# Moving the first pair's x and the third pair's keys in a fused attention and two-layer MLP kernel on one Trainium2 core

## The chip, the cores and the metric

The kernel runs on one core of one Trainium2 chip. The metric is device time in microseconds (us). Five engines work side by side, each on its own instructions in its own order: TensorE (PE, the matrix engine, whose weight loads are listed apart as PEld), VectorE (DVE), ScalarE (ACT), GpSimd (POOL) and SyncE (SP). SP issues nearly all DMAs here, GpSimd a few. A matrix product ends in PSUM, of which this program uses eight banks of 128 x 512 float32; the other engines read it there.

## The reference

```
k_sum = max of k over blocks of 32 keys;  v_sum = mean of v over the same blocks     (batch 2, heads 8, sequence 768, head size 64)
scores = [ q k^T / 8 where |i - j| < 16, else -1e9 ;  q k_sum^T / 8 + log 32 ]
a      = exp(scores - row maximum);  a = a / (row sum + 1e-9)
x      = a [v; v_sum], heads side by side                                             (1536 tokens x 512)
x      = ((x w_a) * (x w_b)) w_out                                                    (inner width 1536)
out    = leaky(x w_in) w_out2, leaky(h) = max(0.01 h, h)                              (inner width 2048)
```

All inputs and outputs are float32.

## The kernel before

**Attention.** Heads are taken two by two (`hp` 0 to 3). Queries are taken 256 at a time, and two such groups make a "pair" `i`. The 1536 tokens are three chunks of 512. The first chunk is pairs 0 to 3, and pair `i` there is head pair `i` of batch 0 with its first 512 queries; "first pair" is pair 0, "third pair" is pair 2. A head pair's keys are loaded once (`load_k`), transposed on TensorE and copied into `kts` by ScalarE, and VectorE takes the maximum of each block of 32 (`k_prep`, whose reduction is L623); GpSimd then copies the maxima beside the windows (L630). Per pair the steps are: `q_prep`, and twice `scores` (16 small products; then on VectorE a masked minimum, L684, and on ScalarE the exponential, L690), `normal` (three VectorE instructions, L699 to L701) and `p_transpose` (four transposes and a ScalarE copy, L715), and at last `pv`, the products with the values (L725). `pv` ends in x: ScalarE rounds the result to the first of two float32r parts (L735) and VectorE subtracts to get the second (L736). The values' windows come by `load_vw`, the block means by `v_sums`, `v_place` and `put_sums`.

**Products with weights.** Each large product is made three times (`mm3`, L743): high by high, high by low, low by high. A weight of 512 KB is loaded by `stage` into one of three buffers (`wst`) and made into two parts by a row of small steps (`convert`): on VectorE L388, on ScalarE the absolute value L394, on VectorE L400, L403 and L409, on ScalarE the high half L416, on VectorE the rest L419. `wc` and `wr`, the tiles between, have two buffers each; a buffer of `wst` is free after L409. The first four weights are two blocks of `w_a` and two of `w_b`, in the order a, b, a, b. As soon as a pair's x is there, `early` multiplies it with all four, into four banks of their own. The other four banks (t0 to t3) go round among the steps of attention.

**What sets the order.** `attention_ops` gives each step a place on a scale (8 per pair, `PER`; `PV` = 13 is where `pv` stands), and the steps are listed by it. After a listed product the loop sends out two more steps of the weights' conversion (`tick(2)`), and `first_weights` sends out all that its weight still needs. The list is the order of priority only: when the program is built, a planner with costs of its own puts each engine's instructions in order, and takes the first on the list among those that it thinks ready. `tc.issue_after(ins)` puts the instructions of its block behind `ins` in the order of the engine on which `ins` runs, if they run on that engine. Once built, the order is fixed. DMAs on SP are ordered in the same way.

## Time and profile before

| | us |
|---|---|
| median of 3 runs | 637.85 |
| lowest, highest | 636.07, 638.39 |
| the profiled execution | 635.28 |
| its span, first to last instruction | 633.4 |

| engine | busy us in the span |
|---|---|
| PE | 611.6 |
| DVE | 485.4 |
| ACT | 317.9 |
| POOL | 55.7 |

The profile is of one execution. A line of a timeline has the start, the duration, the engine, the line of the program, the operation, the tile written and the tiles read, and how many like instructions were merged; in brackets stands how long the engine was idle before it and what ended that. DMA lines (SPq) show the issue, not the transfer; the time to the landing is asked for apart. A busy TensorE isn't TensorE at its peak, since its instructions overlap and their ends are modelled. The clock column gives the share of full speed that TensorE was granted.

### The profile page before, as it was taken

To read this page: it belongs to the slowest core of one execution; us is meant where nothing else is said; L and a number is where in the kernel's file an instruction comes from. 1 tells how busy PE (TensorE), PEld (TensorE's weight loads), DVE (VectorE), ACT (ScalarE), POOL (GpSimd) and SP (SyncE) were. 2 spreads that over 40 slices of the span, in tenths; PEclk is the share of its full clock that TensorE was granted. 3 is DMA by queue.
4 is the path that set the end of the run, shared out by engine and by line. 5 is a ranking of instruction groups with operands and counts; after the bars stand their busy time and mean duration, and the time that the engine had idled before them with its cause. 6 is when DMAs were issued, how large, how long until landed. Compare 5 with 4: busy or idle time off the path is not lost.

```text
span 633.4 us, 9456 instructions
## 1 busy us (share of the span) xinstructions
PE 611.6 (97%) x3344; PEld 498.5 (79%) x3344; DVE 485.4 (77%) x1070; ACT 317.9 (50%) x707; POOL 55.7 (9%) x101
## 2 busy tenths in 40 slices
PE   6589999999999999999999999999999999999997
PEld 4467777777888888888888888877888888888886
DVE  4996987853996869986889999687588576885552
ACT  5677885752545425434453648475463434443320
POOL 5224010000000001202120102000000000000000
PEclk9899999999999999999999999999999999999999
DMA  8989757620124503736593327323133013030013
GB/s 200 257 208 199 160 116 177 191 72 24 45 71 145 136 15 94 139 120 146 142 222 102 89 80 166 95 64 109 35 99 100 14 54 99 1 99 1 0 68 132
DMA packets 81006, 67.85 MB, mean 107 GB/s; under 512 B 47360, under 2 KB 67840, under 8 KB 80960
## 3 DMA queue, kind: packets, MB, share of 16 engines
q1 hardware_dynamic: 75808, 57.95, 31.7%
q0 software_dynamic: 5152, 9.31, 8.8%
q8 instruction: 26, 0.43, 0.3%
q14 instruction: 20, 0.16, 0.1%
HBM read 52.82 MB, written 10.49 MB: 100 GB/s over the span
## 4 chain that ended last, share of the span: by engine, by line
PE 80%; DVE 5%; DMA 5%; ACT 4%; issue 3%; SPq 1%; POOL 1%; POOLq 0%; DVEq 0%; ACTq 0%
PE ps_t L743 34%; PE ps_c L743 17%; PE ps_a L743 12%; PE ps_b L743 11%; PE ps_t L670 2%; DMA wst<-in_moe_w_out_dram 2%; PE ps_t L725 1%; PE ps_t L711 1%; ACT pm L690 1%; DMA neg<-wc 1%; DMA wst<-in_moe_w_a_dram 1%; DVE wc L403 1%; DMA q<-in_q_dram 1%; DVE wc L409 1%; SPq L209 1%
## 5 line engine op out<-in xcount | busy, mean ns | idle before, releaser
L743 PE MATMUL ps_c<-wsp,hs 128*128 128x512 f32 x288 | 75.1, 390 | 1.4 <-ACT acc L860 1.0
L743 PE MATMUL ps_t<-wsp,hs 128*128 128x512 f32 x288 | 74.5, 389 | 0.0
L743 PE MATMUL ps_t<-ys,wsp 128*128 128x512 f32 x270 | 68.2, 389 | 0.0
L394 ACT ACTIVATE wc<-wst 128x512 f32<-128x512 f32 x68 | 45.3, 673 | 45.2 <-DVE wsp L419 17.8
L743 PEld LDWEIGHTS ps_c<-wsp,hs 128*128 128x128 f32 x288 | 53.9, 188 | 13.3 <-ACT acc L860 1.4
L871 DVE TENSOR_TENSOR hs<-h,hs 128x512 fp32r<-128x512 f32 x72 | 49.3, 687 | 18.6 <-ACT hs L870 18.3
L743 PEld LDWEIGHTS ps_t<-wsp,hs 128*128 128x128 f32 x288 | 54.1, 188 | 11.2
L743 PEld LDWEIGHTS ps_t<-ys,wsp 128*128 128x128 f32 x270 | 50.7, 188 | 10.5
L870 ACT CAST hs<-h 128x512 fp32r<-128x512 f32 x72 | 44.5, 621 | 26.0 <-DVE h L1134 18.4
L416 ACT CAST wsp<-wc 128x512 fp32r<-128x512 f32 x68 | 41.8, 620 | 30.6 <-DVE wc L409 30.6
L743 PE MATMUL ps_a<-x,wsp 128*128 128x512 f32 x186 | 51.2, 403 | 4.5 <-ACT x L735 4.1
L743 PE MATMUL ps_t<-x,wsp 128*128 128x512 f32 x222 | 53.2, 389 | 0.0
L743 PE MATMUL ps_b<-x,wsp 128*128 128x512 f32 x192 | 51.7, 398 | 0.0
L1086 DVE TENSOR_TENSOR h<-ps_t,h 128x512 f32<-128x512 f32 x56 | 37.6, 687 | 17.0 <-PE ps_t L743 16.7
L1022 ACT ACTIVATE h<-h 128x512 f32<-128x512 f32 x32 | 20.2, 632 | 57.5 <-DVE h L1086 57.4
L743 PEld LDWEIGHTS ps_t<-x,wsp 128*128 128x128 f32 x222 | 41.7, 188 | 8.6
L403 DVE SCALAR_TENSOR_TENSOR wc<-wc,wr 128x512 int32<-128x512 int32 x68 | 46.5, 686 | 0.7
L409 DVE SCALAR_TENSOR_TENSOR wc<-wst,wc 128x512 int32<-128x512 int32 x68 | 46.6, 686 | 0.6
L743 PEld LDWEIGHTS ps_a<-x,wsp 128*128 128x128 f32 x186 | 33.9, 188 | 13.4 <-ACT x L735 4.6
L419 DVE TENSOR_TENSOR wsp<-wc,wsp 128x512 fp32r<-128x512 f32 x56 | 38.7, 697 | 5.8 <-ACT wsp L416 5.8
L743 PE MATMUL ps_t<-hs,wsp 128*128 128x512 f32 x144 | 42.7, 389 | 0.0
L690 ACT ACTIVATE pm<-pm,nb 128x128 f32<-128x128 f32 x96 | 37.5, 393 | 10.1 <-DVE nb L684 10.0
(129 smaller groups left out, 1098.1 us busy)
## 6 DMA issues: line engine op xcount, KB each, us to landing
wst<-in_moe_w_out_dram SPq DMA_DIRECT2D x28, 512.0 KB, 3.4
wst<-in_moe_w_in_dram SPq DMA_DIRECT2D x16, 512.0 KB, 3.8
wst<-in_moe_w_a_dram SPq DMA_DIRECT2D x12, 512.0 KB, 4.8
wst<-in_moe_w_b_dram SPq DMA_DIRECT2D x12, 512.0 KB, 4.0
y<-acc POOLq DMA_DIRECT2D x16, 256.0 KB, 6.1
y<-acc SPq DMA_DIRECT2D x12, 256.0 KB, 2.3
neg<-wc POOLq DMA_DIRECT2D x12, 256.0 KB, 3.5
acc<-y SPq DMA_DIRECT2D x12, 256.0 KB, 3.1
```

The lines of the kernel that those rows point to most:

```text
L394: nc.scalar.activation(out=t["c"].bitcast(F32), in_=hi_w.bitcast(F32), func=AF.Abs, scale=2.0**-112)
L403: nc.vector.scalar_tensor_tensor(out=t["c"], in0=t["c"], scalar=3, in1=t["r"], op0=ALU.logical_shift_left, op1=ALU.bitwise_or,)
L409: nc.vector.scalar_tensor_tensor(out=t["c"], in0=hi_w, scalar=SIGN, in1=t["c"], op0=ALU.bitwise_and, op1=ALU.bitwise_or,)
L416: t["high"] = nc.scalar.copy(out=t["w"][:, 0], in_=t["c"].bitcast(F32))
L419: nc.vector.tensor_tensor(out=t["w"][:, 1], in0=t["c"].bitcast(F32), in1=t["w"][:, 0].bitcast(F32), op=ALU.subtract,)
L670: nc.tensor.matmul(out=ps[h, w, :], lhsT=qt[h, w * W : (w + 1) * W], rhs=kts[h, (g * G + w) * SC : (g * G + w) * SC + P], start=True, stop ...
L690: nc.scalar.activation(out=pm[:, w, :], in_=pm[:, w, :], func=AF.Exp, scale=-1.0, bias=nb[:, w : w + 1], accum_out=sm[:, w : w + 1],)
L743: nc.tensor.matmul(out=ps, lhsT=w(a), rhs=x(b), start=first and j == 0, stop=last and j == 2)
L870: pace["split"] = nc.scalar.copy(out=t[:, 0], in_=src)
L871: nc.vector.tensor_tensor(out=t[:, 1], in0=src, in1=t[:, 0].bitcast(F32), op=ALU.subtract)
L1022: nc.scalar.activation(out=h, in_=src, func=AF.Prelu, alpha=0.01)
L1086: nc.vector.tensor_tensor(out=out, in0=ps, in1=u, op=ALU.add)
```

## The change

- The third pair's keys (batch 0, `hp` 2) are loaded later in the list: after two of the first three weights, which were loaded as three in a row (the third follows the keys).
- Their transposes stand at 13.5 and 13.75 on the scale, behind the first pair's `pv` (they stood at 4 and 5); the fourth pair's, formerly at 13.5 and 13.75, at 14 and 14.25. On TensorE both go behind the last product of values so far.
- Their reductions go behind the subtraction that makes the low part of the first x, and so does the first instruction of the second pair's second `normal`.
- The absolute value (L394) of every weight after the first goes behind the rounding of the first x on ScalarE, where it went behind the placing of the block means.
- Before place 13 only the first weight is converted (five before). The other three of the first four are asked for at 13.5, behind the first `pv`, not at 13 in front of it.

```diff
-                    add(-22 if b > 0 and hp >= NP - 2 else -18, LOAD, load_k, b, hp)
+                    add(-22 if b > 0 and hp >= NP - 2 else -13.4 if (b, hp) == (0, 2) else -18, LOAD, load_k, b, hp)
                     for j in range(2):
-                        add(2 * m + j / 4 - 10.5 if (b, hp) == (0, NP - 1) else 2 * m + j - 12, PRODUCT, k_prep, b, hp, j)
+                        at = {(0, 2): j / 4 - 2.5, (0, 3): j / 4 - 10}.get((b, hp), 2 * m + j - 12)
+                        add(at, PRODUCT, k_prep, b, hp, j)
...
-            with tc.issue_after(pace["turned"].ins):
+            with tc.issue_after(pace["turned"].ins if i < 1 else pace["first x"].ins):
                 nc.scalar.activation(
                     out=t["c"].bitcast(F32), in_=hi_w.bitcast(F32), func=AF.Abs, scale=2.0**-112
                 )
...
-        with tc.issue_after(st["out"].ins) if (b, hp) == (0, NP - 1) else nullcontext():
+        with tc.issue_after(st["out"].ins) if b == 0 and hp >= 2 else nullcontext():
             for i in range(n * GT // P):
                 nc.tensor.transpose(
...
-        nc.vector.tensor_reduce(
-            out=ks_t[hp][:, g * GT // BLK : (g + n) * GT // BLK],
...
+        with tc.issue_after(st["low x"].ins) if (b, hp) == (0, 2) else nullcontext():
+            nc.vector.tensor_reduce(
+                out=ks_t[hp][:, g * GT // BLK : (g + n) * GT // BLK],
...
-        with behind(i == 0):
+        after = st["low x"].ins if (i, j) == (1, 1) else line[-1]
+        with tc.issue_after(after) if i == 0 or (i, j) == (1, 1) else nullcontext():
             nc.vector.tensor_scalar_add(sm, sm, 1.0e-9)
...
-            nc.scalar.copy(out=x[:, 0], in_=src)
-            nc.vector.tensor_tensor(
+            hi = nc.scalar.copy(out=x[:, 0], in_=src)
+            lo = nc.vector.tensor_tensor(
                 out=x[:, 1], in0=src, in1=x[:, 0].bitcast(F32), op=ALU.subtract
             )
+            if i == 0:
+                pace["first x"], st["low x"] = hi, lo
...
-    ops.append((2.5, LOAD, lambda: [stage() for _ in range(3)], 0))
+    ops.append((2.5, LOAD, lambda: [stage() for _ in range(2)], 0))
+    ops.append((2.7, LOAD, stage, 0))
     firsts = ((("a", 0), "a"), (("b", 0), "b"), (("a", 1), "c0"), (("b", 1), "c1"))
     for i, x in enumerate(firsts):
-        ops.append((PV, LOAD, lambda x=x: first_weights(*x), 0))
+        ops.append((PV if i < 1 else PV + 0.5, LOAD, lambda x=x: first_weights(*x), 0))
...
-            if o[1] == PRODUCT and o[0] >= PER+0.5 and (bg or cnt["conv"] < N_FIRST):
+            n_now = 1 if o[0] < PV else N_FIRST
+            if o[1] == PRODUCT and o[0] >= PER+0.5 and (bg or cnt["conv"] < n_now):
                 tick(2)
```

## Rows read from the trace of the kernel before

**Rows 1.** Page, part 1: busy us, share of the span, instructions
```profile
PE 611.6 (97%) x3344; PEld 498.5 (79%) x3344; DVE 485.4 (77%) x1070; ACT 317.9 (50%) x707; POOL 55.7 (9%) x101
```

**Rows 2.** Windows: length, busy us per engine (instructions), granted clock, DMA share, GB/s
```profile
12.00:32.00 20.00, 11.91 (x123) 9.07 (x121) 19.71 (x59) 13.64 (x48) 3.54 (x4) 0.91 0.91 241
...
34.00:47.30 13.30, 11.17 (x113) 8.52 (x112) 13.27 (x45) 10.55 (x35) 3.30 (x4) 1.00 0.79 195
47.30:62.60 15.30, 14.25 (x148) 10.94 (x147) 10.66 (x44) 11.03 (x42) 6.77 (x9) 1.00 0.93 199
62.60:82.00 19.40, 19.25 (x217) 15.37 (x215) 17.30 (x64) 15.81 (x55) 3.44 (x7) 1.00 0.71 154
```

**Rows 3.** Timeline of TensorE around the first large product
```profile
22.52 0.69 PE L725 MATMUL ps_t<-pt,vw 128*64 128x64 f32 x16 [0.99 <-ACT pt L715]
23.15 0.87 PE L612 MATMUL ps_t<-ident,k 128*128 128x128 f32 x6
27.67 0.80 PE L743 MATMUL ps_a<-x,wsp 128*128 128x512 f32 x1 [3.64 <-ACT x L735]
...
29.67 1.67 PE L670 MATMUL ps_t<-kts,qt 64*64 64x128 f32 x16
```

**Rows 4.** Timeline of ScalarE around the first x and the fourth weight
```profile
24.72 0.62 ACT L416 CAST wsp<-wc 128x512 fp32r<-128x512 f32 x1 [0.20 <-DVE wc L409]
26.47 0.68 ACT L394 ACTIVATE wc<-wst 128x512 f32<-128x512 f32 x1 [1.13 <-DVE wsp L419]
27.05 0.57 ACT L735 CAST x<-ps_t 128x512 fp32r<-128x512 f32 x1
...
33.09 0.67 ACT L394 ACTIVATE wc<-wst 128x512 f32<-128x512 f32 x1 [3.16 <-DMA wst<-in_moe_w_b_dram]
```

**Rows 5.** Timeline of VectorE, 15 to 35 us
```profile
15.21 1.01 DVE L623 TENSOR_REDUCE ks<-ps_t 128x16 f32<-128x512 f32 x2
...
16.75 0.39 DVE L699 TENSOR_SCALAR sm<-sm 128x4 f32<-128x4 f32 x1
...
24.94 0.16 DVE L699 TENSOR_SCALAR sm<-sm 128x4 f32<-128x4 f32 x1
...
28.55 0.68 DVE L736 TENSOR_TENSOR x<-ps_t,x 128x512 fp32r<-128x512 f32 x1
...
31.29 0.68 DVE L409 SCALAR_TENSOR_TENSOR wc<-wst,wc 128x512 int32<-128x512 int32 x1
33.03 0.43 DVE L388 TENSOR_SCALAR wr<-wst 128x512 int32<-128x512 uint32 x1 [1.07 <-DMA wst<-in_moe_w_b_dram]
33.80 0.43 DVE L400 TENSOR_SCALAR wc<-wc 128x512 f32<-128x512 f32 x1 [0.34 <-ACT wc L394]
34.14 0.28 DVE L684 CUSTOM_DVE_ANT_0 pm<-ps_t,negm_first 128x128 f32<-128x128 f32 x1
```

**Rows 6.** Timeline of SP: issues of DMAs
```profile
6.97 0.98 SPq L146 DMA_DIRECT2D k<-in_k_dram  x2
...
14.14 0.51 SPq L364 DMA_DIRECT2D wst<-in_moe_w_a_dram  x1
...
24.36 0.92 SPq L181 DMA_DIRECT2D vb<-in_v_dram  x2
...
26.95 0.37 SPq L364 DMA_DIRECT2D wst<-in_moe_w_b_dram  x1
```

**Rows 7.** Tile k, issue at 6.97 alone: time to landing
```profile
DMA to landing us min/median/max: 5.9/5.9/5.9
```

**Rows 8.** Timeline of GpSimd: the copy of the third pair's maxima
```profile
16.29 0.83 POOL L630 COPY kts<-ks 128x288 f32<-128x288 f32 x1 [5.52 <-DVE ks L623]
```

**Rows 9.** Tile wst, issue at 26.95 alone: time to landing
```profile
DMA to landing us min/median/max: 6.1/6.1/6.1
```

**Rows 10.** Windows: first and last of four in which TensorE's clock fell
```profile
27.50:28.00 0.50, 0.33 (x1) 0.34 (x2) 0.50 (x3) 0.50 (x2) 0.00 (x0) 0.50 1.05 320
...
30.00:31.00 1.00, 1.00 (x14) 1.00 (x12) 1.00 (x3) 0.00 (x0) 0.00 (x0) 0.55 1.10 351
```

More of the change, by code (lines that the diff above doesn't have):

```diff
@@ L622, in k_prep @@
         )
-        nc.vector.tensor_reduce(
-            out=ks_t[hp][:, g * GT // BLK : (g + n) * GT // BLK],
-            in_=ps[:, : n * GT].rearrange("p (n j) -> p n j", j=BLK),
-            op=ALU.max,
-            axis=AX.X,
-        )
+        with tc.issue_after(st["low x"].ins) if (b, hp) == (0, 2) else nullcontext():
+            nc.vector.tensor_reduce(
+                out=ks_t[hp][:, g * GT // BLK : (g + n) * GT // BLK],
+                in_=ps[:, : n * GT].rearrange("p (n j) -> p n j", j=BLK),
+                op=ALU.max,
+                axis=AX.X,
+            )
         if g + n == NGB:
```

## The prediction

> **What bounds the kernel now.** I read the page's busy shares first, then the stretches (busy time of each engine in windows), then the timelines of the engines where the stretches showed idle time. Over the whole span TensorE is the bound: 611.6 of 633.4 us [rows 1]. But nearly all of what it loses, it loses early. Between 12 and 32 us it is busy for 11.91 of 20 us, while from 62.6 to 82 us it is busy for 19.25 of 19.40 [rows 2]; so from 62.6 us on, whatever is won or lost before stays to the end. The reader should see in the same rows which engine is full where TensorE is not: VectorE, 19.71 of 20 us from 12 to 32 and 13.27 of 13.30 from 34 to 47.3. In the stretch after that it has slack (10.66 of 15.30) and TensorE is nearly full (14.25). So up to 47 us the kernel moves at VectorE's pace, and afterwards at TensorE's.
>
> The timelines show two places where this start-up stumbles. First, TensorE ends its transposes at 24.0 us (the group that starts at 23.15) and then stands 3.64 us until ScalarE has rounded the first pair's x, to start the first large product at 27.67 [rows 3]. On ScalarE that rounding (27.05) stood behind an absolute value of the third weight at 26.47, which had itself waited 1.13 us for VectorE [rows 4]. Secondly, VectorE waits 1.07 us at 33.03 for the fourth weight's DMA and 0.34 more at 33.80 for that weight's absolute value [rows 5]. ScalarE stood 3.16 us for the same DMA [rows 4].
>
> **The change part by part.** *Loads.* The third pair's two key DMAs (0.98 us of issue at 6.97) leave their place, and everything that SP has behind them up to the second weight issues about 1.0 us sooner: weight 1 at 13.1 in place of 14.14 [rows 6]. The keys then issue behind weights 1 and 2, at some 13.1 + 2 x 0.51 = 14.1 [rows 6]; the queue held the first of them 5.9 us in the old place [rows 7], so it would land at 20.0 and the second at 20.5. Weight 3 and the fourth pair's keys keep their times, because in front of them stands the same list in another order. The keys' new reader comes behind the first products of values, which end at 22.52 + 0.69 = 23.21 now [rows 3]: even 1.0 us sooner, at 22.2, that covers both landings by more than 1.5 us, and if that cover goes, TensorE waits there for as much as is missing.
>
> *The third pair's preparation.* Two reductions (1.01 us at 15.21) leave VectorE's front part, and with them four copies on ScalarE and a 0.83 us copy on GpSimd [rows 5, 8]. So the first products of values can end up to 1.0 us earlier, at 22.2 at best. The reductions come back behind the subtraction of the first x: the total on VectorE is unchanged.
>
> *x in a given place.* The absolute values of the second weight onward now wait behind the rounding of x. What is queued behind them on ScalarE are those weights' high halves, the key copies of pairs three and four and the copy of turned probabilities; VectorE waits for the first, TensorE for the others. Without the 26.47 instruction and its 1.13 us wait, x follows at latest the high half of weight 1, which ends at 24.72 + 0.62 = 25.34 [rows 4], and that less the 1.0 us of the part before is 24.3. The other bound is the end of the products, 22.2. I take 24.3, because the old order put the exponentials and that high half first. The first large product then starts near 24.3 + 0.6 = 24.9, 2.8 us sooner; the subtraction moves from 28.55 to about 24.9 as well [rows 3, 5]. The 1.0 us of the second pair's normalisation that is put behind it costs nothing: the subtraction now comes before the time at which that work stood.
>
> *Transposes of pairs three and four* (0.87 us for the six at 23.15, so twice that) follow the first products of values and fill TensorE where it was empty [rows 3]. Their cost is nothing as long as x is the later one.
>
> *What this is worth.* Up to weight 4 VectorE has the same instructions to do as before, in another order, and was full; so it reaches weight 4 near 32 us again, whatever TensorE gained. There its wait can go. Weight 4's DMA was issued at 26.95, once weight 1 had given back its buffer, and needed 6.1 us [rows 6, 9]. Weight 1 is converted alone now and gives it back 1 to 2 us sooner, but SP has the values at 24.36 and the queries in front. The issue is then bounded by 24.4 and 26.95, the landing by 30.5 and 33.05. I take the middle of the two, 25.7, which lands at 31.8, just ahead of VectorE. Then the 1.07 and 0.34 us go: 1.41 us. What is late next is VectorE itself.
>
> The shift is kept through 47.3 (VectorE full), then by TensorE. I count nothing for TensorE's earlier products, since VectorE's next work on the third pair's scores stood at 34.14, while those scores had started on TensorE at 29.67 [rows 3, 5].
>
> A granted clock of 0.50 (the 1.2 GHz level) shows from 27.5 to about 30.9 us, after TensorE's pause [rows 10]. The scores made in it waited for VectorE anyway, so the row gives me no term. The Trainium skill ("TensorE: Matmul & The Clock Gate", Terms) puts the price of throttled time at that time times one minus the rate: by it 3.4 x 0.5 = 1.7 us would come on top, and the sum would be 3.1 us. No row says which holds; that possibility is in the first rival.
>
> Against the change speaks GpSimd's copy of the keys. At its old place the add beside it took 0.39 us, where the same add takes 0.16 [rows 5, 8]: 0.23 us go there, and at the new place 0 to 0.83 us can be lost. I take no difference. The Trainium skill ("SBUF — State Buffer", Who interferes with whom) says that a VectorE instruction with two SBUF inputs and a GpSimd instruction that reads SBUF block each other; the new neighbours are of that kind, so by it the gain would be 1.41 + 0.23 - 0.83 = 0.8 us.
>
> **The sum.** The profiled execution took 635.28 us, 633.4 of span and 1.9 around it. 635.28 - 1.41 = 633.87. The median shown is 637.85, 2.57 above the profiled one; on that footing the forecast is 637.85 - 1.41 = 636.4 us. Its own range, with weight 4 as late as before (0) or twice the gain (2.8, as much as the first product moves), is 635.0 to 637.9.
>
> **Rivals.** *TensorE's gain comes through whole.* For it: TensorE is the bound over the span, and the second pair's turned probabilities and x hang on its order as much as on VectorE. Against it: VectorE is full in the same stretch. Price: 2.8 us of earlier products and 1.7 us of half clock, 4.5 us: 633.35.
>
> *Slower: the third pair's keys come too late.* The reductions stand in VectorE's order behind the pieces of weights 2 to 4 as the program lists them. Two weights cost no delay: each is two pieces of 0.43 us (as at 33.03 and 33.80) and three of 0.68 (as at 31.29) [rows 5], 2.9 us, and 24.9 + 0.7 + 5.8 = 31.4 is still before weight 4. It turns where the reductions fall behind the fourth weight's first piece, at 33.03: then 33.03 + 2.9 + 1.01 + 0.83 + 1.67 (reductions, copy, scores) = 39.4 against 34.14, 5.3 us, of which VectorE can bridge at most half with other work. Price 2.7 to 5.3, middle 4: 641.9. For it speaks that this DMA was late already; against it that the reductions are ready some 7 us sooner.
>
> *The change doesn't do what it says:* x stays behind the exponentials and weight 4 lands as late as before. Nothing moves after 33 us: 637.85.
>
> **How the numbers follow.** Chances: forecast 0.44, whole gain 0.28, late keys 0.13, no effect 0.15. About 0.5% (3.2 us) is what a measurement of this kernel can tell from no change, so the borders are 634.7 and 641.0. Faster: about 0.8 of the whole gain (0.22), plus the forecast's tail (0.07) and 0.02 of the rest, 0.31. Slower: most of the late keys (0.10) and 0.03 for an order of the later work that I can't see, 0.13. The rest, 0.56, is within. The range 632.4 to 640.6 leaves out below about a quarter of the whole-gain case (0.07) and above two thirds of the late keys (0.09).
>
> **What would show it.** In the profile after: the rounding of the first x near 24.3 and the first large product near 24.9; no stretch at 0.50 near 28 us; the third pair's reductions between 25 and 31 us; the fourth weight's first piece on VectorE without a wait, before 32.5. If VectorE leaves its full stretch at about 46 in place of 47.3 us and the end follows by as much, the forecast is right. If the second x already comes 3 us sooner, and VectorE is not full before 32, the first rival holds. A pause of VectorE near 34 us for the third pair's scores shows the second. A wait of 1 us on weight 4 again with all ends in place shows the third. I am wrong altogether if the time changes with all of these as forecast: then the order of the work after 47 us has changed, which the trace of before can't show.

## The result and the profile after

The kernel after takes 642.81 us (median of 4 runs, 642.65 to 643.57), the kernel before 637.03 (4 runs beside it, 636.07 to 638.39): a ratio of 1.0091, 95% interval [1.0067, 1.0115]. It is slower by 5.8 us, outside the range of the forecast (632.4 to 640.6) and on the other side of no change. The profiled execution took 642.65 us with a span of 640.4. The profiled execution of the kernel before had a span of 633.4, at 635.28 us a quick one of its kind, so the two profiles lie 7.0 us apart, more than the medians.

Busy time over the span, and the four stretches that stand in [rows 1, 2] (length, busy us of each engine with instructions, granted clock, DMA share, GB/s), now of the kernel after:

```profile
PE 617.7 (96%) x3344; PEld 502.4 (78%) x3344; DVE 483.9 (76%) x1070; ACT 317.6 (50%) x707; POOL 54.6 (9%) x101
```

```profile
12.00:32.00 20.00, 13.57 (x120) 10.28 (x121) 17.16 (x51) 12.58 (x45) 3.38 (x4) 0.74 0.94 240
...
34.00:47.30 13.30, 10.18 (x80) 6.81 (x80) 11.03 (x37) 7.40 (x25) 1.77 (x2) 0.76 0.65 157
47.30:62.60 15.30, 14.87 (x134) 11.80 (x133) 8.55 (x39) 9.83 (x34) 6.38 (x8) 0.94 1.02 219
62.60:82.00 19.40, 18.86 (x184) 14.90 (x182) 17.26 (x57) 15.36 (x54) 3.26 (x6) 1.00 0.56 118
```

VectorE, which was full up to 47 us, no longer is: 17.16 of 20 us and 11.03 of 13.30. One longer stretch gives the size of the loss. The same view from 24 to 62 us, of the kernel before:

```profile
24.00:62.00 38.00, 31.18 (x296) 23.54 (x296) 31.95 (x108) 26.35 (x89) 10.23 (x13) 0.96 0.90 213
```

And of the kernel after:

```profile
24.00:62.00 38.00, 32.10 (x245) 23.23 (x246) 26.13 (x89) 21.70 (x72) 8.72 (x12) 0.78 0.88 199
```

VectorE does 31.95 - 26.13 = 5.8 us less work in the same time (the two spans differ by 7.0 us). TensorE is no less busy than before (32.10 against 31.18), but at a lower clock and with some 50 instructions fewer, so its busy time says nothing here.

The start went as forecast. On TensorE the first pair's `pv` ends at 21.7 us, and the first large product starts at 24.74 (27.67 in [rows 3]):

```profile
21.02 0.69 PE L728 MATMUL ps_t<-pt,vw 128*64 128x64 f32 x16 [0.60 <-ACT pt L718]
...
24.74 0.49 PE L747 MATMUL ps_a<-x,wsp 128*128 128x512 f32 x1
...
28.15 1.12 PE L714 MATMUL ps_t<-ident,pm 128*128 128x128 f32 x4 [1.14 <-DVE ks L625]
```

Then VectorE comes to the fourth weight too early and finds it later than before (answers to [rows 5]; L389 is the first piece of a weight, L410 the join, L420 the rest):

```profile
29.55 1.01 DVE L625 TENSOR_REDUCE ks<-ps_t 128x16 f32<-128x512 f32 x2
...
34.09 0.43 DVE L389 TENSOR_SCALAR wr<-wst 128x512 int32<-128x512 uint32 x1 [3.53 <-DMA wst<-in_moe_w_b_dram]
34.44 0.69 DVE L410 SCALAR_TENSOR_TENSOR wc<-wst,wc 128x512 int32<-128x512 int32 x1
35.04 0.69 DVE L420 TENSOR_TENSOR wsp<-wc,wsp 128x512 fp32r<-128x512 f32 x1
...
40.82 0.43 DVE L389 TENSOR_SCALAR wr<-wst 128x512 int32<-128x512 uint32 x1 [2.18 <-DMA wst<-in_moe_w_a_dram]
```

3.53 us in place of 1.07. Behind it now stand two pieces that stood in front of it before: the join of the third weight (31.29 in [rows 5]) and the rest of the second, in the kernel before at

```profile
29.75 0.68 DVE L419 TENSOR_TENSOR wsp<-wc,wsp 128x512 fp32r<-128x512 f32 x1
```

And there are 2.18 us more for the fifth weight, for which the kernel before did not wait. SyncE's timeline shows why the fifth is late (answers to [rows 6]): value windows, queries and value blocks stand in front of it.

```profile
26.69 0.44 SPq L365 DMA_DIRECT2D wst<-in_moe_w_b_dram  x1
27.23 4.41 SPq L209 DMA_DIRECT2D vw<-in_v_dram  x6
31.68 3.82 SPq L156 DMA_DIRECT2D q<-in_q_dram  x4
35.54 0.46 SPq L176 DMA_DIRECT2D vb<-in_v_dram  x1
36.12 0.37 SPq L365 DMA_DIRECT2D wst<-in_moe_w_a_dram  x1
```

The waits of SyncE from 26 to 37 us (what it waited for, us in total, times, longest) show what held it longest there: by the profile, the queries stood until the fourth weight had landed.

```profile
SPq L156 <- DMA wst<-in_moe_w_b_dram: 1.9, 1, 1.9
```

The fourth weight's DMA, asked for alone, took 7.4 us, against 6.1 in [rows 9]:

```profile
DMA to landing us min/median/max: 7.4/7.4/7.4
```

On ScalarE (answers to [rows 4]) the second pair's x is rounded at 45.91, though its products ended at 41.0 on TensorE. It stands behind the absolute value of the fifth weight, four exponentials and the high half of the fourth weight:

```profile
24.12 0.56 ACT L738 CAST x<-ps_t 128x512 fp32r<-128x512 f32 x1
...
35.16 0.62 ACT L417 CAST wsp<-wc 128x512 fp32r<-128x512 f32 x1 [4.75 <-DVE wc L410]
...
40.88 0.67 ACT L395 ACTIVATE wc<-wst 128x512 f32<-128x512 f32 x1 [2.05 <-DMA wst<-in_moe_w_a_dram]
...
45.39 0.62 ACT L417 CAST wsp<-wc 128x512 fp32r<-128x512 f32 x1 [0.98 <-DVE wc L410]
45.91 0.58 ACT L738 CAST x<-ps_t 128x512 fp32r<-128x512 f32 x1
```

In the kernel before, ScalarE came to the same instruction at 38.73, behind one exponential:

```profile
37.78 0.66 ACT L394 ACTIVATE wc<-wst 128x512 f32<-128x512 f32 x1 [0.70 <-DVE wsp L419]
38.34 0.39 ACT L690 ACTIVATE pm<-pm,nb 128x128 f32<-128x128 f32 x1
...
38.73 0.56 ACT L735 CAST x<-ps_t 128x512 fp32r<-128x512 f32 x1
```

So the roundings of the four x give stations by which all kernels can be compared. After them comes the first `g` copy; from there to the end of the span it took 571.2 to 574.9 us in all twenty kernels, so what decides is over at 61 to 73 us.

| kernel | first x | second | third | fourth | first g | span | ratio to before, 95% |
|---|---|---|---|---|---|---|---|
| before | 27.05 | 38.73 | 50.12 | 58.58 | 61.26 | 633.4 | 1 |
| after | 24.12 | 45.91 | 56.81 | 64.97 | 67.64 | 640.4 | 1.0091 [1.0067, 1.0115] |
| e1_loads | 33.11 | 47.60 | 56.50 | 64.46 | 67.13 | 641.4 | 1.0114 [1.0085, 1.0143] |
| e2_keys | 26.36 | 41.34 | 53.70 | 61.39 | 64.06 | 636.8 | 1.0059 [1.0037, 1.0082] |
| e3_convert | 25.79 | 43.78 | 55.57 | 63.56 | 66.28 | 638.2 | 1.0069 [1.0043, 1.0095] |
| e4_no_convert | 25.81 | 43.70 | 56.03 | 64.21 | 66.87 | 641.8 | 1.0067 [1.0042, 1.0092] |
| e5_no_loads | 25.21 | 45.84 | 56.08 | 64.62 | 67.29 | 638.8 | 1.0107 [1.0079, 1.0136] |
| h1_fill | 24.30 | 45.23 | 56.23 | 65.28 | 67.95 | 639.2 | 1.0119 [1.0094, 1.0144] |
| g2_fifth | 24.78 | 44.07 | 56.30 | 67.19 | 69.86 | 642.6 | 1.0100 [1.0060, 1.0141] |
| g3_fourth_fifth | 24.80 | 39.87 | 52.58 | 63.21 | 65.98 | 638.5 | 1.0076 [1.0051, 1.0101] |
| g4_seventh | 24.54 | 39.62 | 50.21 | 63.48 | 66.24 | 638.9 | 1.0080 [1.0055, 1.0105] |
| i4_aside | 24.35 | 48.27 | 60.86 | 69.67 | 72.44 | 645.0 | 1.0114 [1.0081, 1.0147] |
| k4_after_join | 25.39 | 46.74 | 58.10 | 66.36 | 69.04 | 641.9 | 1.0096 [1.0067, 1.0125] |
| k1_g2_aside | 24.99 | 39.90 | 54.11 | 64.33 | 67.10 | 638.7 | 1.0087 [1.0054, 1.0120] |
| j1_after_half | 24.65 | 45.42 | 55.01 | 63.17 | 65.84 | 637.9 | 1.0069 [1.0043, 1.0094] |
| j3_after_pool | 23.70 | 41.05 | 61.03 | 70.50 | 73.19 | 646.3 | 1.0206 [1.0177, 1.0235] |
| i3_noconv_fourth | 25.29 | 40.24 | 55.82 | 63.98 | 66.75 | 638.8 | 1.0096 [1.0059, 1.0133] |
| i2_before_fourth | 28.23 | 41.44 | 52.73 | 61.68 | 64.42 | 638.4 | 1.0036 [1.0013, 1.0059] |
| j2_before_half | 27.24 | 40.44 | 51.56 | 61.08 | 63.75 | 637.1 | 1.0028 [1.0009, 1.0048] |
| j4_before_pool | 27.75 | 39.38 | 50.20 | 61.60 | 64.27 | 637.2 | 1.0045 [1.0029, 1.0060] |

Stations and spans are of one execution each, the ratios of all runs. A station can be off by as much as the executions of a kernel differ. In e4, for one, three took 637.1 to 638.9 us and nine 640.5 to 644.1, and the profiled one is the longest of all; the profiled one of i3 is the shortest of its six.

### The profile page after: what moved, and what is told of

It is laid out like the page before. It is cut to its first block, busy times and chain, and to the rows that moved or that the text cites. A ratio compares the mean times of both kernels' runs of the same rounds, so it can differ in the third digit from the quotient of the medians.

```text
span 640.4 us, 9457 instructions
## 1 busy us (share of the span) xinstructions
PE 617.7 (96%) x3344; PEld 502.4 (78%) x3344; DVE 483.9 (76%) x1070; ACT 317.6 (50%) x707; POOL 54.6 (9%) x101
## 3 DMA queue, kind: packets, MB, share of 16 engines
q1 hardware_dynamic: 75808, 57.95, 31.8%
## 4 chain that ended last, share of the span: by engine, by line
PE 80%; DMA 7%; DVE 5%; issue 3%; ACT 3%; SPq 1%; POOLq 0%; DVEq 0%; ACTq 0%
PE ps_t L747 33%; PE ps_c L747 18%; PE ps_a L747 12%; PE ps_b L747 11%; PE ps_t L672 2%; DMA neg<-wc 2%; DMA wst<-in_moe_w_a_dram 2%; PE ps_t L714 1%; PE ps_t L728 1%; ACT pm L692 1%; DMA wst<-in_moe_w_b_dram 1%; DVE h L1092 1%; DMA vb<-in_v_dram 1%; DMA q<-in_q_dram 1%; DVE wc L404 1%
## 5 line engine op out<-in xcount | busy, mean ns | idle before, releaser
L410 DVE SCALAR_TENSOR_TENSOR wc<-wst,wc 128x512 int32<-128x512 int32 x68 | 46.6, 687 | 0.5
L389 DVE TENSOR_SCALAR wr<-wst 128x512 int32<-128x512 uint32 x68 | 28.6, 423 | 21.2 <-ACT wsp L436 9.4
L747 PE MATMUL ps_c<-hs,wsp 128*128 128x512 f32 x144 | 42.4, 390 | 0.3 <-DVE acc L869 0.3
```

Source lines behind the costliest of these rows:

```text
L389: nc.vector.tensor_scalar(out=t["r"], in0=lo_w.bitcast(U32), scalar1=2.0**-29, scalar2=7.0, op0=ALU.mult, op1=ALU.min,)
L410: nc.vector.scalar_tensor_tensor(out=t["c"], in0=hi_w, scalar=SIGN, in1=t["c"], op0=ALU.bitwise_and, op1=ALU.bitwise_or,)
L747: nc.tensor.matmul(out=ps, lhsT=w(a), rhs=x(b), start=first and j == 0, stop=last and j == 2)
```

## The experiments

An edit leaves the planner free to put the rest in another order. Where an experiment kept the order of some engines, it says so.

**The parts of the change by themselves.** Before with the loads alone; with the third pair's keys, the reductions and the normalisation alone; with the conversions and the absolute values alone; and after without that last part.

```diff
e1,e4 -add(-22 if b > 0 and hp >= NP - 2 else -18, LOAD, load_k, b, hp)
e1,e4 +add(-22 if b > 0 and hp >= NP - 2 else -13.4 if (b, hp) == (0, 2) else -18, LOAD, load_k, b, hp)
e1,e4 +ops.append((2.7, LOAD, stage, 0))                          # two in a row before it, not three
e2,e4 +at = {(0, 2): j / 4 - 2.5, (0, 3): j / 4 - 10}.get((b, hp), 2 * m + j - 12)
e2,e4 +with tc.issue_after(st["low x"].ins) if (b, hp) == (0, 2) else nullcontext():    # reductions; one add too
e3    +with tc.issue_after(pace["turned"].ins if i < 1 else pace["first x"].ins):       # absolute values
e3    +ops.append((PV if i < 1 else PV + 0.5, LOAD, lambda x=x: first_weights(*x), 0))
e3    +n_now = 1 if o[0] < PV else N_FIRST
```

> The kernel before with the loads alone changed: the third pair's keys behind two weights, the third weight behind them. Theory A (the fifth weight's load, late because weights 2 to 4 are converted behind x): no part of the loss is here, 635 to 638 us. Theory B (TensorE's clock: in the profile after it stands at half rate for 20.5 us, 3.4 before): no loss unless the clock falls for longer; the loss should be about half of the added half-clock time, here 0 to 1 us. Theory C (the third pair's keys come too late): some of the loss, 1 to 2 us, since the keys land 7 us later.

> The kernel before with the third and fourth pairs' transposes behind the first products of values, the third pair's reductions and the second pair's second normalisation behind the first x's subtraction; loads and weights as before. Theory A: within 1.5 us of before, 636 to 638.5. Theory B: slower where the clock falls for longer, by half of the added half-clock time, up to 6 us. Theory C: most of the loss is here, 640 to 643 us.

> The kernel before with the weights' conversion alone changed: the absolute values of weights 2 on behind the rounding of the first x, those weights asked for behind the first products of values. Theory A: most of the loss is here, 640 to 643 us, and the profile shows the fifth weight's DMA issued at 35 us or later (28.67 before, 36.12 after), with VectorE and ScalarE waiting for it. Theory B: loss only as half of added half-clock time. Theory C: no loss, 634 to 637 us.

> The changed kernel with the weights' conversion put back as before: loads and third pair's keys stay changed. Theory A: the loss goes, 635 to 638 us. Theory B: it goes as far as the half-clock stretches go; a long one that stays should keep half its length. Theory C: the loss stays, 640 to 643 us.

Measured: 644.16, 640.25, 641.08 and 642.73 us, before 637.49. Each part is slower alone, and they don't add up. In e1 the third pair's transposes, left in their old place on TensorE, run at 20.46 in place of 13.43, and the first x (33.11) comes behind an absolute value that waited for VectorE, as before the change. TensorE itself waited only 0.37 us there for the keys' landing, so how much of the delay is theirs isn't shown. e3 alone shows the waits of the kernel after, 2.14 us on weight 4 and 2.07 on weight 5; in e4 the fifth weight is on time (issued at 31.64) and the wait on the fourth stays, 2.42 us. So the conversion part is what makes the fifth weight late. Neither theory A (all of the loss is the fifth weight; against it e1, e2 and e4) nor theory C (all of it is the third pair's keys; against it e3) is left whole. Theory B, the clock, is taken up at the end.

**The loads' part taken back, the clock, and the fifth weight's place.** After with the old order of loads; after with 20 small bfloat16 products on TensorE in its pauses, the order of all other work unchanged on all engines; after with the third pair's value windows behind the fifth weight on SP, the order of TensorE and ScalarE unchanged; and that with the second half of the value blocks and the fourth pair's queries behind the fourth weight as well (here ScalarE's order changes too: the second x is rounded ahead of the fourth weight's high half).

```diff
e5 -the three e1 lines above, taken out of the kernel after
h1 +ops.append((8.1, SIDE, lambda: fill(3, ("scored", 1, 0)), 0))    # and 8, 9 products behind the keys' transposes
g2 +with tc.issue_after(pace["w", 5].ins) if (b, hp) == (0, 2) else nullcontext():        # load_windows
g3 +with tc.issue_after(pace["w", 4].ins) if i == 3 else behind_values(i in (4, 5, 6, 7)):  # load_q
g3 +with tc.issue_after(pace["w", 4].ins) if i == 1 else nullcontext():                    # load_vb
```

> The changed kernel with the loads in the old order (the third pair's keys ahead of the weights): the keys' and the weights' parts stay. Theory A: the fifth weight is as late as in the changed kernel, so the loss stays, 641 to 644 us. Theory B: the loss is half of the added half-clock time, whatever that is. If the delayed loads themselves are the cause, 636 to 639 us.

> The changed kernel with 20 idle products on TensorE (bf16, 256 columns of the identity, into the bank that the fourth weight uses later): 3 after the second pair's first scores, 8 after the third pair's transposes, 9 after the fourth pair's. The order of all other work on every engine is that of the changed kernel. Theory B (the loss is TensorE's half-rate clock, a consequence of the pauses at 13, 22.5 and 27 us): the stretch at half rate from 25 to 39 us goes or shrinks, and the time falls by about half of what goes, to 637 to 640 us. Theory A (the fourth and fifth weights' DMAs hold VectorE and ScalarE, and TensorE waits for them): the clock may rise, but the waits on the DMAs stay, 642 to 644 us.

> The changed kernel with one thing moved on SP: the third pair's windows of values are issued behind the fifth weight, which therefore goes out at about 30 us and not at 36.1. The order on the other engines is that of the changed kernel. Theory A: VectorE and ScalarE no longer wait 2 us for that weight at 41, the second x comes up to 5 us sooner, 637 to 640 us. Theory B: the clock stretches stay as they are and so does the time, 642 to 644 us.

> As before this one, and the fourth weight is issued ahead of the values' and queries' loads that stood in front of it (near 24.6 us, not 26.7). Theory A: the 3.5 us wait of VectorE at 34 us goes too, 635 to 639 us, the best of these. Theory B: 641 to 644 us unless the clock stretches shorten.

e5: 642.34 us, with waits of 2.55 and 2.00 us: the loads' order is not the cause. h1: 643.40. Its windows (as in [rows 2]) show the clock full from 10 to 30 us:

```profile
10.00:20.00 10.00, 7.01 (x89) 5.24 (x87) 8.79 (x36) 6.99 (x28) 2.42 (x5) 1.00 1.01 246
20.00:30.00 10.00, 6.46 (x68) 4.59 (x62) 9.96 (x29) 7.08 (x25) 1.13 (x2) 1.00 0.83 192
```

VectorE of h1 waits for both weights as in the kernel after:

```profile
33.65 0.43 DVE L389 TENSOR_SCALAR wr<-wst 128x512 int32<-128x512 uint32 x1 [2.93 <-DMA wst<-in_moe_w_b_dram]
...
40.13 0.43 DVE L389 TENSOR_SCALAR wr<-wst 128x512 int32<-128x512 uint32 x1 [1.94 <-DMA wst<-in_moe_w_a_dram]
```

The kernel after itself had, in the same view of windows:

```profile
15.00:18.00 3.00, 2.93 (x17) 2.44 (x18) 2.97 (x15) 1.18 (x2) 0.00 (x0) 0.50 1.02 327
...
25.00:27.00 2.00, 1.77 (x5) 0.82 (x4) 2.00 (x7) 2.00 (x8) 0.00 (x0) 0.55 0.91 178
```

The second x of h1 comes at 45.23, 0.7 us sooner than in the kernel after, though the clock is at 1.00 up to 30 us and, after a dip to 0.66, from 35 to 40 us as well (0.61 in the kernel after). So the low clock isn't what makes the second x late. What the low clock costs after that h1 doesn't show, because there it comes back later: 0.57 from 40 to 52 us, where the kernel after has 0.86. The windows of h1:

```profile
35.00:40.00 5.00, 3.83 (x49) 2.55 (x47) 3.20 (x12) 3.39 (x12) 0.96 (x1) 1.00 0.73 230
40.00:52.00 12.00, 8.85 (x43) 7.01 (x44) 9.81 (x34) 6.75 (x18) 4.61 (x5) 0.57 0.74 173
```

And of the kernel after:

```profile
40.00:52.00 12.00, 8.88 (x66) 6.86 (x66) 9.72 (x34) 6.01 (x16) 5.34 (x6) 0.86 0.75 173
```

g2: 642.64 us; the fifth weight is issued at 30.88 and not waited for, but VectorE's 2.78 us on the fourth stay and the second x comes at 44.07. g3: 640.52 us; neither weight is waited for, and the second x comes at 39.87, 6.0 us earlier than in the kernel after. Of these 6.0 us, 4.3 are gone by the fourth x. The timeline of ScalarE in g3 shows the next wait, on the seventh weight:

```profile
39.87 0.56 ACT L740 CAST x<-ps_t 128x512 fp32r<-128x512 f32 x1
...
49.52 0.66 ACT L397 ACTIVATE wc<-wst 128x512 f32<-128x512 f32 x1 [3.20 <-DMA wst<-in_moe_w_a_dram]
...
52.58 0.57 ACT L740 CAST x<-ps_t 128x512 fp32r<-128x512 f32 x1
```

**One weight's place on VectorE; the next load; the same on the kernel before.**

```diff
i4 +with tc.issue_after(pace["rest"].ins) if i == 3 else nullcontext():     # first piece of the fourth weight, in after
g4 +with tc.issue_after(pace["w", 2 * hp + 1].ins) if (b, hp) in ((0, 2), (0, 3)) else nullcontext():  # in g3
g4 +with tc.issue_after(pace["w", 7].ins) if i == 1 else behind_values(True):                          # second value blocks
i2 +the two g3 lines, in the kernel before
i3 +the two g3 lines, in e4
```

> The kernel after, with one order changed: VectorE's first piece of the fourth weight is held behind the two joins and the remainder of the third weight, so that it no longer stands ahead of work that is ready (it now follows the minima of the third pair's first tile and the first sum of value blocks too). The loads keep their order. Theory A (VectorE stands behind a weight that has not landed; the loss is the work queued behind it): the wait of 3.53 us on the fourth weight goes to under 0.5 us, ScalarE's high half of the third weight comes some 3.5 us earlier, the second pair's x is rounded 2 to 4 us earlier than 45.9 us, and the time falls by 1.5 to 3.5 us to 639.3-641.3. Theory C (the landing of the weights themselves sets the pace, whatever stands in front of it): the wait goes, but the second pair's x stays at 45-46 us and the time at 642-643.

> The kernel after with the fourth and fifth weights' loads ahead (as in the run before of that kind, 640.5), and now the seventh weight's load ahead of the second half of the values and of the fourth pair's value windows as well; only SyncE's order is changed against that run, TensorE, VectorE and ScalarE keep theirs. Theory A (what was left there, 12.7 us from the second x to the third in place of 11.4, is the same kind of wait, ScalarE's 3.20 us on the seventh weight at 49.5 us): the seventh weight is issued near 40 us in place of 42.95, that wait falls to under 1.5 us, the third x comes 1.5 to 3 us earlier, and the time falls by another 1.5 to 3 us to 637.5-639. Theory D (the order in which the engines' work was put is the loss, and moving loads only moves the wait): the fourth pair's value windows or another load become late, and the time stays at 640-641.

> The kernel before with the fourth weight's load put ahead of the second half of the value blocks and of the fourth pair's queries on SyncE. Theory A (waits on landing weights are what can be won or lost here): the fourth weight is issued near 24.3 us in place of 26.95, lands near 30.5, VectorE's waits of 1.07 and 0.34 us and ScalarE's of 3.16 us go, the second x comes 1 to 1.5 us earlier than 38.73, and the time falls by 0.7 to 1.5 us below the kernel before. Theory D: the order that follows on the engines is another one and takes the gain back: within 0.7 us of the kernel before or slower.

> The change without its part on the conversions (the early x, the third pair's keys and the loads are in; 642.7 as it was run), and with the fourth weight's load ahead of the second half of the value blocks and of the fourth pair's queries. Theory A (there the waits were VectorE's 2.42 us and ScalarE's 5.39 us on the fourth weight alone): the waits go, the second x comes 2 to 4 us earlier than 43.7, and the time falls to 638.5-640.5. Theory D: the waits go and the time stays at 641.5-643.

i4: 644.99 us, slower than either theory expected. The wait on the fourth weight is gone, and VectorE meets the fifth, issued at 36.43 as in the kernel after, so much earlier (its timeline in i4):

```profile
43.18 0.43 DVE L390 TENSOR_SCALAR wr<-wst 128x512 int32<-128x512 uint32 x1 [7.57 <-DMA wst<-in_moe_w_a_dram]
```

g4: 643.27 us (639.75 to 645.56). The seventh weight is issued at 40.40 and its wait is gone; the third x comes at 50.21, as early as before the change. But the queries behind it on SP are now late, TensorE waits for them, and the fourth x is at 63.48, not at 58.58 (timeline of TensorE in g4):

```profile
51.65 0.41 PE L653 MATMUL ps_t<-ident,q 128*128 128x128 f32 x2 [1.61 <-DMA q<-in_q_dram]
53.36 0.41 PE L653 MATMUL ps_t<-ident,q 128*128 128x128 f32 x2 [1.30 <-DMA q<-in_q_dram]
```

i2: 639.66 us, slower than the kernel before by 1.0036 [1.0013, 1.0059], against the expectation. The planner answered the earlier load by putting the fourth weight's first piece further forward on VectorE, ahead of the first x's subtraction, which now stands behind the DMA (28.55 in [rows 5]; VectorE's timeline in i2):

```profile
31.72 0.43 DVE L389 TENSOR_SCALAR wr<-wst 128x512 int32<-128x512 uint32 x1 [1.89 <-DMA wst<-in_moe_w_b_dram]
32.06 0.69 DVE L737 TENSOR_TENSOR x<-ps_t,x 128x512 fp32r<-128x512 f32 x1
```

i3: 643.25 us; the second x at 40.24 instead of 43.70, as expected, and the third at 55.82: 15.6 us later, and by the fourth x 0.2 us of the gain are left. VectorE's wait on the fourth weight did not go as expected: 2.33 us of it are left, but they end at 29.16, not at 34.77 as in e4. So for the second x it matters when VectorE gets past the weight, more than how long it stood.

**Bytes or the queue.** After and before with half the bytes of weights 4 to 8 (VectorE keeps its order but for two pieces in j1; in j2 some more move), and with these weights' loads issued by GpSimd.

```diff
j1,j2 +n = KT // 2 if 4 <= cnt["st"] <= 8 else KT       # zeros by GpSimd in the other half
j3,j4 +put = nc.gpsimd if 4 <= cnt["st"] <= 8 else nc.sync
```

> The kernel after with the second half of the columns of the staging tile of weights 4 to 8 not loaded (256 KB of 512 KB each); GpSimd writes zeros there instead, so the products of these weights are not the reference's. The instructions on the engines keep their number and nearly their order (two pieces of VectorE change places with a neighbour). Theory F (the loads are the limit: what the 16 DMA engines, 0.9 busy from 10 to 65 us, and SyncE's one queue can bring by a given time decides when each x is ready): 1.28 MB less to bring, the waits of 3.53 and 2.18 us on weights 4 and 5 fall to under 1 us each, the second x comes before 42 us, and the time falls by 4 to 7 us to 636-639. Theory D (the order on the engines is the loss, whatever the loads): the waits go but the second x stays after 44 us and the time at 641-643.

> The kernel before with the same halves of weights 4 to 8 not loaded (zeros by GpSimd in their place). Theory F: its waits on weight 4 (1.07 and 3.16 us) go, the x of the fourth pair comes 2 to 3 us earlier, the time falls by 1 to 3 us to 634-636, and the distance to the kernel after treated in the same way shrinks from 5.8 us to under 3. Theory D: the distance stays at 5 to 6 us.

> The kernel after with the loads of weights 4 to 8 issued by GpSimd instead of SyncE; the bytes are the same, TensorE, VectorE and ScalarE keep their order but for two or three neighbours. Theory F1 (what makes the weights late is SyncE's order: each stands behind queries and value blocks that wait for a buffer): weights 4 and 5 are issued as soon as their buffers are free, near 24-27 and 29-31 us, the wait of 2.18 us on weight 5 goes, the one on weight 4 falls under 2 us, and the time falls by 2 to 5 us to 638-641. Theory F2 (the rate of the 16 DMA engines is what is short): whatever comes earlier makes something else later, and the time stays within 1.5 us of 642.8.

> The kernel before with the loads of weights 4 to 8 issued by GpSimd instead of SyncE; the order on VectorE, ScalarE and TensorE is somewhat another one. Theory F1: faster than the kernel before by 0.5 to 2 us, since its waits on weight 4 go. Theory F2: within 1 us of it. Theory D (any other order than that of the kernel before costs): slower by 2 us or more.

j1: 640.76 us, its interval overlapping that of the kernel after. VectorE waited for the fourth weight as long as in the kernel after:

```profile
34.24 0.43 DVE L392 TENSOR_SCALAR wr<-wst 128x512 int32<-128x512 uint32 x1 [3.43 <-DMA wst<-in_moe_w_b_dram]
```

For 256 KB took nearly as long to land as 512 KB had, counted from its issue at 26.90:

```profile
DMA to landing us min/median/max: 7.2/7.2/7.2
```

The wait on the fifth weight did fall, to 0.99 us, and the second x still came at 45.42. So the bytes to be brought explain some 2 us of 5.8, if any. j2: 638.87 us, slower than the kernel before with fewer bytes to bring, again with the fourth weight's first piece put forward on VectorE and a wait of 2.11 us there; and TensorE waits 1.73 us for GpSimd's copy of the block means, which the zeros on GpSimd may have made late. j3: 649.47 us. Both waits fall (0.84 us is left on the fifth), and the second x comes at 41.05. But the seventh weight then stands on GpSimd behind additions of value blocks, is issued only at 50.22, and ScalarE waits 11.10 us for it. GpSimd's timeline in j3, and then ScalarE's:

```profile
50.22 1.03 POOL L366 DMA_DIRECT2D wst<-in_moe_w_a_dram  x1
```

```profile
56.67 0.66 ACT L396 ACTIVATE wc<-wst 128x512 f32<-128x512 f32 x1 [11.10 <-DMA wst<-in_moe_w_a_dram]
```

j4: 639.57 us, slower by 1.0045 [1.0029, 1.0060]. VectorE has no wait on the fourth weight left, and the third x (50.20) is where it was before. Then ScalarE stands behind the seventh weight, which GpSimd issues at 48.87 in place of SyncE's 42.10:

```profile
55.39 0.66 ACT L395 ACTIVATE wc<-wst 128x512 f32<-128x512 f32 x1 [3.03 <-DMA wst<-in_moe_w_a_dram]
```

**Two neighbours, and both waits.** After with the third weight's join ahead of the fourth weight's first piece, ScalarE's and SyncE's order unchanged; and g2 with the edit of i4.

```diff
k4 +with tc.issue_after(pace["join"].ins) if i == 3 else nullcontext():
k1 +with tc.issue_after(pace["rest"].ins) if i == 3 else nullcontext():     # in g2
```

> The kernel after with two neighbours on VectorE exchanged: the join of the third weight, which was queued right behind the first piece of the fourth weight, now goes ahead of it (and on TensorE two products by the second columns go ahead of two others); ScalarE and SyncE keep their order, the loads too. Theory A2 (the place of a weight's first piece on VectorE decides what its late landing holds up): the join comes at about 30.6 us in place of 34.44, ScalarE's high half of the third weight at about 31.3 in place of 35.16, the wait on the fourth weight falls from 3.53 to about 2.5 us; the wait of 2.18 us on the fifth weight stays; the time falls by 0.7 to 2.5 us. Theory E (the landings of the fourth and the fifth weight carry the rest by themselves): the high half comes earlier, the second x stays at 45-46 us and the time within 0.7 us of 642.8.

> The kernel after with both waits of VectorE taken by order: the fourth weight's first piece behind the third weight's joins and remainder (as in the run where it alone was moved, 645.0, and VectorE stood 7.57 us behind the fifth weight instead), and the fifth weight's load ahead of the third pair's value windows on SyncE. Theory A2: both waits fall under 1.5 us together, the second x comes before 43 us, and the time is 638.5-641. Theory E: VectorE's waits move on to the next weights or to another load and the time stays at 641.5-645.

k4: 643.43 us. The join comes at 31.73 instead of 34.44, ScalarE's high half at 32.44 instead of 35.16, and it brings nothing, since VectorE still waits for both landings (its timeline in k4):

```profile
34.92 0.43 DVE L390 TENSOR_SCALAR wr<-wst 128x512 int32<-128x512 uint32 x1 [2.52 <-DMA wst<-in_moe_w_b_dram]
...
41.65 0.43 DVE L390 TENSOR_SCALAR wr<-wst 128x512 int32<-128x512 uint32 x1 [2.78 <-DMA wst<-in_moe_w_a_dram]
```

k1: 642.46 us. VectorE waits on neither weight and the second x comes at 39.90. From there to the fourth x it takes 24.4 us (19.1 in the kernel after, 19.9 before): ScalarE waits 2.42 us for the seventh weight, and TensorE 2.22 us for GpSimd's copy into the third pair's windows. ScalarE's timeline in k1, and then TensorE's:

```profile
39.90 0.56 ACT L740 CAST x<-ps_t 128x512 fp32r<-128x512 f32 x1
...
46.89 0.69 ACT L397 ACTIVATE wc<-wst 128x512 f32<-128x512 f32 x1 [2.42 <-DMA wst<-in_moe_w_a_dram]
```

```profile
50.28 0.69 PE L730 MATMUL ps_t<-pt,vw 128*64 128x64 f32 x16 [2.22 <-POOL vw L225]
```

## Why the prediction was wrong

*Right: what bounds, and the start.* The first x at 24.12 (forecast 24.3), the first large product at 24.74 (24.9), the third pair's reductions from 27.41 to 30.6. They weren't quite free, as I had them: TensorE stood 1.14 us behind one of them at 28.15. GpSimd's copy of the maxima cost VectorE nothing, as the sum took it: the join beside it (28.95) took 0.68 us, as elsewhere. And what is lost by 62.6 us stays: the end follows the first `g` by 572 us, give or take 3, in every kernel.

*Failed, the step that carried the sum: "which lands at 31.8, just ahead of VectorE".* Both halves of it were wrong. The DMA was issued at 26.69, not 25.7: weight 1 gave its buffer back at 22.0, 2.7 us sooner than before, but SP reached the load only behind the values and queries. And it took 7.4 us, not 6.1, to about 34.1; why longer isn't shown. VectorE did not reach weight 4 "near 32 us again" but at 30.56, because two pieces of about 0.7 us each that I counted in front, the third weight's join and the second's rest, had been put behind. The wait that was to go, 1.41 us, became 3.53.

*Not in the sum: the fifth weight.* I followed one load and stopped there. The change's conversion part, by itself (e3) and in the whole, moved the fifth weight on SP behind queries and value blocks, from 28.67 to 36.12 us, and that cost VectorE 2.18 us more. The two waits make 5.71 us against 1.41: 4.3 of the 5.8 us that VectorE did less between 24 and 62 us.

*The rivals.* "TensorE's gain comes through whole" fell with the second x, 7.2 us later in place of 3 earlier. "The third pair's keys come too late" gave nearly the right time, 641.9, for a reason that didn't occur. It is the same mechanism one step on: VectorE behind a DMA, with ready work queued behind it.

*The clock.* I gave it no term, and forecast no stretch at 0.50 near 28 us; there is one, from 25 to 39 us. It isn't what makes the second x late, as h1 shows. What it costs behind the second x is open. Over all executions the clock goes with the time: its mean over the span is 0.992 in the 91 executions of the kernel before that stand beside the experiments, and 0.984 in the four of the kernel after. But other kernels don't keep to it. j1 has 0.984 too and is 4.0 us slower than the kernel before, i3 has 0.989 and is 6.4 us slower, and h1, with 0.987, is no faster than the kernel after. A low clock can be a mark of TensorE's pauses as well as a cause of time, and no run held it up through 62 us with the rest unchanged.

The Trainium skill ("TensorE: Matmul & The Clock Gate", Terms) prices time at the low clock at its length times one minus the rate. By that price, as an estimate from the mean clocks above, the executions of the kernel before lose 4.9 us and those of the kernel after 10.1, and the difference of 5.2 us is most of the loss. For i3 the same estimate gives 2.1 us of 6.4. So the runs neither bear the price out nor refute it.

*What is shown.* The late second x comes from VectorE standing behind the fourth and the fifth weight, both of them. Without these waits it comes at 39.6 to 41.1 us, in three ways: by loads (g3, and g4 built on it), by a load and an order (k1), by another queue (j3). In g3 and k1 ScalarE's order changed as well (there the second x goes ahead of a high half), in j3 not at this place. Taking the wait on one weight alone doesn't do it: with the fifth on time the second x is at 44.07 (g2) and 43.70 (e4), and with the fourth put aside at 48.27, since VectorE then stands behind the fifth (i4). Shown as well: an early second x does not bring the time back. In all twelve variants that keep at least two of the change's three parts (e4, e5, i3 and the nine built on the whole change), the fourth x stayed at 63.17 us or later, against 58.58. What had been won by the second x went again where the next wait showed: on the seventh weight (g3, k1, j3), on the queries (g4), on GpSimd's copy (k1, j3). Not the cause of the late second x: the loads' order (e5), the low clock (h1), the neighbour behind the wait (k4). The bytes explain at most some 2 us of the time (j1).

*What is open.* What keeps the fourth x of these kernels 4.6 us or more behind that of the kernel before isn't shown. One candidate is the order of the work on VectorE and ScalarE as the planner leaves it, another the lower clock above. For the order speaks that the kernel before with an earlier load (i2), where the planner changed that order, was slower too. j2 and j4 say less, because GpSimd had more to do in both, and j4's loss shows only behind the seventh weight. The order of before was not held while the loads were changed, so this is argued and not shown. In the letters of the expectations from i4 on: A and F1 hold up to the second x and fall for the time, F holds for at most a third of it, F2 for neither j3 nor j4, E for the times of k4 and k1, and D fits the time but was not isolated. No variant beat the kernel before.

## What to carry to other kernels

When a change lets an engine arrive earlier at a load, list what stood in front of that load and is now behind it, and follow the loads after it through the issuing queue, not only the next one. A wait is worth its length only if no other load or engine is due within that length; here removing 5.7 us of waits moved a station by 6 us and the end by 2. In this kernel's start the loads follow each other closely, each due within 1 to 3 us of its reader, and there an edit that brought its own station sooner still lost.

## What the runs showed of the hardware

- A DMA's time to landing did not follow from its size alone. The fourth weight took 7.4 us with 512 KB (kernel after) and 7.2 us with 256 KB (j1), with a DMA share of 1.05 and 1.00 over those stretches. The fifth, issued at 36.1 and 36.2 us, took 4.7 and 3.1 us, at 0.88 and 0.86. What was queued ahead was not varied by itself.
- TensorE stayed at a granted clock of 0.51 (the 1.2 GHz level) from 30 to 39 us in the kernel after, while by the profile it was busy for the whole of it, mostly with small products. Twenty small products in its pauses kept it at 1.00 from 10 to 30 us (h1); there it fell later, to 0.57 from 40 to 52 us. The window of the kernel after:

```profile
30.00:39.00 9.00, 9.00 (x45) 6.00 (x45) 5.11 (x16) 4.08 (x13) 0.42 (x1) 0.51 0.84 187
```
